# Gated spectral mix with MLP, forward and gradients: opening in blocks of four row tiles with the gate on TensorE, FFT first stage spread over the next pass, edge columns batched, loads paced

## Chip, cores, metric

The kernel runs on one core of a Trainium2 chip. The metric is the time of one execution on the device in microseconds (us).

The engines go by the names of the profile: PE multiplies and transposes matrices, DVE, ACT and POOL work on vectors, and SP issues most of the loads (SPq is its queue). PE writes its results into PSUM tiles; ACT or DVE then copies them out, which the text calls evacuation. The granted clock is the share of its full clock that PE was given.

## The reference, cut to what matters

```python
# x, grad_out: (2048, 1024) bf16;  w1: (1024, 3584);  w2: (3584, 1024)
g = sigmoid((x * gate_w).sum(-1, keepdims=True))
a = irfft2(rfft2(x) * (w_r + 1j * w_i))           # spectral branch
r = relu(x @ w1 + b1);  b = (r * r) @ w2 + b2     # MLP branch
out = g * a + (1 - g) * b                         # forward
# returned: out and the eight gradients with respect to
# x, w_r, w_i, w1, b1, w2, b2 and gate_w, for the given grad_out
```

## The kernel before

The kernel goes through five stages. In the **opening** every tile of 128 rows of `x` is turned (transposed on PE) into `xT`, its gate is computed, and `dbn = grad_out * (1 - gate)` is turned into `dbT`. The **h/dh pass** computes `ph` = w1ᵀx and `pd` = w2·db for 28 feature chunks by 4 row blocks, and turns the results for later. The **gradient GEMMs** (`pw`) have the middle of the FFT (`px`, `pv`) and its inverse stage (`pki`, `pui`) threaded between them. The **output GEMMs** (`acc`, `accg`) end the kernel. Python generators decide the interleaving: a `yield` is a place at which the builder may put another generator's instructions.

The opening took one row tile at a time, with the gate's dot product on DVE, and the FFT's first stage sat in the same generator:

```python
for i0 in range(0, NT, 4):
    ...                                           # cut: four loads xt; b1 loaded and turned
    for i in range(i0, i0 + 4):
        turned(xT, xt, i, nc.scalar.copy)         # 8 PE transposes, ACT evacuates
        nc.vector.tensor_tensor_reduce(out=junk[:], in0=xt[:], in1=gatew_bc[:], ..., accum_out=sgate[:, c_])
        nc.scalar.activation(gcol[:, c_], sgate[:, c_], ACT.Sigmoid)
        nc.vector.tensor_scalar(out=omg[:, c_], in0=gcol[:, c_], scalar1=-1.0, scalar2=1.0, ...)
        ld(out=go[:], in_=go_perm[i])
        nc.vector.tensor_scalar(out=dbn[:, i, :], in0=go[:], scalar1=omg[:, c_], ...)
        turned(dbT, dbn[:, i, :], i, nc.vector.tensor_copy)
    for i in range(i0, i0 + 4):
        one_s1(fb, cf, 0, i, xts[i - i0], kf[:])  # first FFT stage of x
    yield
for i in range(NT):                               # first FFT stage of grad_out * gate
    ...                                           # cut
    one_s1(fb, cf, 1, i, go, kg[:])
    yield
```

One unit of the first stage is a chain over three engines; the inverse stage has the same form with `pki`, `rt`, `pui`:

```python
pk = fps.tile(..., tag="ps2", bufs=2)             # PE: 8 small matmuls
nc.scalar.copy(out=ft[:], in_=pk[:])              # ACT evacuates
pu = fps.tile(..., tag="ps2", bufs=2)
column_stage(FWD, pu, ft, cf)                     # PE: 8 matmuls that read ft
nc.any.tensor_copy(out=u..., in_=pu[:])
```

All PE turns share one pair of PSUM buffers, `tag="tr", bufs=2`. The three other places that the change touches:

```python
# middle of the FFT: edge columns in matmuls of 1 or 2 columns
mm(sp[:, j, 0, :], lhsT=C, rhs=edge(0), ...)      # four such per j in spectrum, three in back
ld(out=z[:], in_=z_scr[T]...)                     # z loaded just ahead of its first use
# gradient GEMMs, at job n == 1: 16 residual loads in one burst
for t in range(NT):
    ld(out=x_[:], in_=x_perm[t])
# output GEMMs, at block k == 1: seven loads of w1T, 1 MB each, in one burst
for fc in range(0, FC, 4):
    ld(out=w1T[:, fc : fc + 4, :], in_=w1T_scr[fc : fc + 4]...)
```

Of the kernel before, what the change touches and what calls it, by code (L numbers as in the profile page):

```python
# [130 lines left out]
def kernel(  # L131
# [63 lines left out]
    ld(out=kf[:], in_=cten["kf"].ap())  # L195
    gatew_bc = pers.tile([P, D], BF16, name="gatew_bc", tag="gatew_bc")
    ld(out=gatew_bc[:], in_=gate_w.partition_broadcast(P))
    b2_bc = pers.tile([P, D], BF16, name="b2_bc", tag="b2_bc")
    cols = lambda n, w, dt=FP32: pers.tile([P] + w, dt, name=n, tag=n)
    sgate, gcol, omg, gpg, aGo, dsc = (cols(n, [NT]) for n in ("sgate", "gcol", "omg", "gpg", "aGo", "dsc"))  # L200
# [13 lines left out]
    ax_scr = [[dram.tile([P, D], FDT, name=f"ax_scr{T}_{i}") for i in range(NT)] for T in range(2)]  # L214

# [58 lines left out]
    def spectrum(fb, T, m, z, mats, sgn):  # L274
# [11 lines left out]
        sp = tps.tile([P, 2, 2, 2], FP32, name="sp", tag="tr", bufs=2)  # L286
        for j in range(2):
            re, im = main[j]
            C, Sn, N = (mats[:, j, a, :] for a in range(3))
            px = fps.tile([P, 2, H], FP32, name="px", tag="ps2", bufs=2)  # L290
            edge = lambda c_: z[:, c_, 0::H]
            mm(px[:, 0, :], lhsT=C, rhs=re, start=True, stop=False)
            mm(px[:, 1, :], lhsT=C, rhs=im, start=True, stop=False)
            kw = dict(skip_group_check=True)
            if m:

                mm(sp[:, j, 0, :], lhsT=C, rhs=edge(0), start=True, stop=False, **kw)
                mm(sp[:, j, 0, :], lhsT=(Sn if j == 0 else N), rhs=edge(1), start=False, stop=True, **kw)
                mm(sp[:, j, 1, :], lhsT=C, rhs=edge(1), start=True, stop=False, **kw)
                mm(sp[:, j, 1, :], lhsT=(N if j == 0 else Sn), rhs=edge(0), start=False, stop=True, **kw)  # L300
            else:
                mm(sp[:, j, 0, :], lhsT=C, rhs=edge(j), start=True, stop=True, **kw)
                mm(sp[:, j, 1, :], lhsT=(N if j == 0 else Sn), rhs=edge(j), start=True, stop=True, **kw)
            mm(px[:, 0, :], lhsT=Sn, rhs=im, start=False, stop=True)
            mm(px[:, 1, :], lhsT=N, rhs=re, start=False, stop=True)  # L305
            (nc.scalar.copy if j == 0 else nc.vector.tensor_copy)(out=x[:, j, :, 0:H], in_=px[:])  # L306
        V(out=x[:, :, :, 0::H], in0=sp[:], in1=sgn[:], op=ALU.mult)
        return x

    def back(fb, T, m, y, mats):  # L310

        v = fb.tile([P, 2, 2, LW], FDT, name="v", tag="v")
        sp = tps.tile([P, 2, 2], FP32, name="si", tag="tr", bufs=2)
        for j in range(2):
            C, Sn, N = (mats[:, j, a, :] for a in range(3))
            yr, yi = y[:, j, 0, :], y[:, j, 1, :]
            pv = fps.tile([P, 2, H], FP32, name="pv", tag="ps2", bufs=2)
            kw = dict(skip_group_check=True)
            mm(pv[:, 0, :], lhsT=C, rhs=yr[:, 0:H], start=True, stop=False)
            mm(pv[:, 1, :], lhsT=C, rhs=yi[:, 0:H], start=True, stop=False)  # L320
            mm(sp[:, j, :], lhsT=C, rhs=y[:, j, :, H], start=True, stop=False, **kw)
            mm(sp[:, j, 1:2], lhsT=Sn, rhs=yr[:, H : H + 1], start=False, stop=False, **kw)
            mm(sp[:, j, 0:1], lhsT=N, rhs=yi[:, H : H + 1], start=False, stop=True, **kw)
            mm(pv[:, 1, :], lhsT=Sn, rhs=yr[:, 0:H], start=False, stop=True)
            mm(pv[:, 0, :], lhsT=N, rhs=yi[:, 0:H], start=False, stop=True)
            (nc.scalar.copy if j == 0 else nc.vector.tensor_copy)(out=v[:, j, :, 0:H], in_=pv[:])
        nc.vector.tensor_copy(out=v[:, :, :, H], in_=sp[:])
        pc = fb.tile([P, 2, 2, H], FDT, name="pc", tag="pc", bufs=2)
        if m:
            V(out=pc[:, 0], in0=v[:, 0, :, 0:H], in1=v[:, 1, :, 0:H], op=ALU.add)  # L330
            vf = v[:].rearrange("p j c l -> p (j c) l")
            V(out=pc[:, 1], in0=vf[:, 3::-3, 0:H], in1=vf[:, 1:3, 0:H], op=ALU.subtract)
            V(out=pc[:, 0, 1, 0:1], in0=v[:, 0, 0, H : H + 1], in1=v[:, 1, 0, H : H + 1], op=ALU.add)
            V(out=pc[:, 1, 1, 0:1], in0=v[:, 1, 1, H : H + 1], in1=v[:, 0, 1, H : H + 1], op=ALU.subtract)
        else:
            nc.vector.tensor_copy(out=pc[:], in_=v[:, :, :, 0:H])
            nc.vector.tensor_copy(out=pc[:, :, 1, 0:1], in_=v[:, :, 0, H : H + 1])
        st(out=y_scr[T][:].rearrange("c p l -> p c l")[:, m : m + 9 : 8, :], in_=pc[:].rearrange("p j c l -> p j (c l)"))

    def fft_mid():  # L340
# [3 lines left out]
        for m in range(S2 // 2):  # L344
            am = pair_mats(fb, "amat", m)
            w = fb.tile([P, 2, 2, LW], BF16, name="w", tag="w", bufs=2)
            for c_, src_w in enumerate((A_w_r, A_w_i)):
                ld(out=w[:, :, c_, 0:W1], in_=rows2(src_w, m))
            xs = []
            for T in range(2):  # L350
                z = fb.tile([P, 2, D], FDT, name="z", tag="z", bufs=2)
                ld(out=z[:], in_=z_scr[T][:].rearrange("c p l -> p c l")[:, m : m + 9 : 8, :])
                xs.append(spectrum(fb, T, m, z, am, sgn))
                yield 8
            ap = pair_mats(fb, "apmat", m)
            wr = w[:, :, 0:1, 0:W1].to_broadcast([P, 2, 2, W1])
            wi = w[:, :, 1:2, 0:W1].to_broadcast([P, 2, 2, W1])
            for T in range(2):
# [5 lines left out]
                y = fb.tile([P, 2, 2, LW], FDT, name="y", tag="y", bufs=2)  # L364
                a_, b_ = (ALU.subtract, ALU.add) if T == 0 else (ALU.add, ALU.subtract)
                V(out=y[:, :, 0, 0:W1], in0=t1_[:, :, 0, 0:W1], in1=t2_[:, :, 1, 0:W1], op=a_)
                V(out=y[:, :, 1, 0:W1], in0=t1_[:, :, 1, 0:W1], in1=t2_[:, :, 0, 0:W1], op=b_)
                back(fb, T, m, y, ap)
                yield 8
# [13 lines left out]
            yield 4  # L383
# [48 lines left out]
    def rows_and_first_stage():  # L432

        fb, fbs = pool("f1", "right")
        cf = fb.tile(list(consts["cf"].shape), FDT, name="cf", tag="cf")
        b1row = fb.tile([FC, P], BF16, name="b1row", tag="b1row")
# [6 lines left out]

        for i0 in range(0, NT, 4):
            xts = []
            for i in range(i0, i0 + 4):
                xt = fb.tile([P, D], BF16, name="xt", tag="xt", bufs=4)
                ld(out=xt[:], in_=x_perm[i])
                xts.append(xt)
            if i0 == 0:  # L450
                ld(out=b1row[:], in_=B_b1.rearrange("(fc p) -> fc p", p=P))
                b1ps = tps.tile([P, FC], BF16, name="b1ps", tag="tr", bufs=2)
                nc.tensor.transpose(b1ps[:], b1row[:], identb[:FC, :FC])
                nc.vector.tensor_copy(out=b1col[:], in_=b1ps[:])
            for i in range(i0, i0 + 4):
                xt = xts[i - i0]
                c_ = slice(i, i + 1)
                turned(xT, xt, i, nc.scalar.copy)
                junk = fb.tile([P, D], BF16, name="junkt", tag="junkt")
                nc.vector.tensor_tensor_reduce(  # L460
                    out=junk[:], in0=xt[:], in1=gatew_bc[:], scale=1.0, scalar=0.0,
                    op0=ALU.mult, op1=ALU.add, accum_out=sgate[:, c_],
                )
                nc.scalar.activation(gcol[:, c_], sgate[:, c_], ACT.Sigmoid)
                nc.vector.tensor_scalar(out=omg[:, c_], in0=gcol[:, c_], scalar1=-1.0, scalar2=1.0, op0=ALU.mult, op1=ALU.add)
                go = fb.tile([P, D], BF16, name="go", tag="go", bufs=3)
                ld(out=go[:], in_=go_perm[i])
                nc.vector.tensor_scalar(out=dbn[:, i, :], in0=go[:], scalar1=omg[:, c_], scalar2=None, op0=ALU.mult)
                turned(dbT, dbn[:, i, :], i, nc.vector.tensor_copy)
            if i0 == 0:  # L470
                ld(out=cf[:], in_=cten["cf"].ap())
            for i in range(i0, i0 + 4):
                one_s1(fb, cf, 0, i, xts[i - i0], kf[:])
            yield
        V(out=gpg[:], in0=gcol[:], in1=omg[:], op=ALU.mult)
        for i in range(NT):
            go = fb.tile([P, D], BF16, name="go", tag="go", bufs=3)
            ld(out=go[:], in_=go_perm[i])
            kg = fb.tile([P, P], FDT, name="kg", tag="kg", bufs=2)
            nc.vector.tensor_scalar(out=kg[:], in0=kf[:], scalar1=gcol[:, i : i + 1], scalar2=None, op0=ALU.mult)  # L480
            one_s1(fb, cf, 1, i, go, kg[:])
            yield
        fbs.close()


    def mlp_in():
# [5 lines left out]
        SW = 512  # L492
        for fp in range(FC // 2):
            w1g = wb.tile([P, DC, PW], BF16, name="w1g", tag="w1g", bufs=2)
            ld(out=w1g[:], in_=w1v[:, :, fp * PW : (fp + 1) * PW])
            h2S = wb.tile([P, NT, PW], BF16, name="h2S", tag="stg", bufs=3)
            dhS = wb.tile([P, NT, PW], BF16, name="dhS", tag="stg", bufs=3)
            for f2 in range(2):
# [288 lines left out]
```

## Time and profile before

| | before |
|---|---|
| time, median of 4 runs | 1483.88 us (1483.01 to 1484.96) |
| span of the profiled execution | 1482.7 us |
| PE work (weight loads times pace) | 1405.9 us |
| lost by PE | 77 us |

"PE work" is the number of PE weight loads in a stretch times the pace at which that kind of matmul follows the last one; the prediction derives the paces. "Lost" is the length of a stretch less its PE work. The page's row of busy times, shares and instruction counts says this of before:

```profile
PE 1426.7 (96%) x8333; PEld 723.4 (49%) x8482; DVE 669.2 (45%) x1319; ACT 438.2 (30%) x564; POOL 219.9 (15%) x395
```

There are 8482 weight loads (PEld) but only 8333 recorded matmuls, which is why the loads are counted.

### The profile page before, as it was taken

How to read it: one execution, taken by the hardware profiler on the slowest of the kernel's cores; microseconds unless marked ns; L12 is line 12 of the kernel's file. 1: busy time of each engine (PE TensorE's matmuls, PEld its weight loads, DVE VectorE, ACT ScalarE, POOL GpSimd, SP SyncE). 2: the span in 40 equal slices, each digit the busy share in tenths (PEclk: the TensorE clock that was granted, in tenths of full speed). 3: DMA queues.
4: the chain of work that ended last, by engine and by line, in shares of the span. 5: the costliest groups of instructions: out<-in, count | busy, mean ns of one | idle time of the engine just before them, and what ended most of it. 6: DMA issues, size and time to landing. Idle time of an engine off the chain costs nothing. (4 is left out here: it accounts for less than half of the span.)

```text
span 1482.7 us, 20756 instructions
## 1 busy us (share of the span) xinstructions
PE 1426.7 (96%) x8333; PEld 723.4 (49%) x8482; DVE 669.2 (45%) x1319; ACT 438.2 (30%) x564; POOL 219.9 (15%) x395
## 2 busy tenths in 40 slices
PE   6899999999999997999999999999989999999998
PEld 4655555555555553444444444444445544444443
DVE  7953343343433335555554443211455655562222
ACT  5854444444444331322322222333222200000000
POOL 1321111111111111111101122111101100000000
PEclk9999999999999999999999999999999999999999
DMA  7565555555555747555546544944785554664430
GB/s 258 165 210 185 184 181 179 171 178 166 180 171 177 280 135 282 185 187 181 167 155 187 186 181 164 336 153 146 240 285 164 161 155 128 182 185 126 122 112 22
DMA packets 157194, 267.45 MB, mean 180 GB/s; under 512 B 10652, under 2 KB 90538, under 8 KB 155306
## 3 DMA queue, kind: packets, MB, share of 16 engines
q1 hardware_dynamic: 122890, 147.59, 31.5%
q0 software_dynamic: 34208, 118.53, 23.8%
q8 instruction: 66, 1.08, 0.3%
q14 instruction: 30, 0.25, 0.1%
HBM read 147.57 MB, written 118.51 MB: 179 GB/s over the span
## 5 line engine op out<-in xcount | busy, mean ns | idle before, releaser
L520 PE MATMUL pd<-dbT,w2T 128*128 128x512 bf16 x883 | 211.5, 379 | 1.7 <-DVE dhT L521 1.0
L514 PE MATMUL ph<-xT,w1g 128*128 128x512 bf16 x850 | 211.6, 379 | 1.4
L521 DVE SCALAR_TENSOR_TENSOR dhT<-pd,rT 128x512 bf16<-128x512 f32 x112 | 77.5, 692 | 275.9 <-PE pd L520 257.8
L677 PE MATMUL acc<-w,hblk 128*128 128x512 bf16 x874 | 198.4, 381 | 1.2
L616 PE MATMUL pw<-grp,res 128*128 128x512 bf16 x870 | 198.2, 379 | 1.3
L604 PE MATMUL pw<-dbn,grp 128*128 128x512 bf16 x872 | 195.5, 379 | 1.2
L715 PE MATMUL accg<-w1Tr,hblk 128*128 128x512 bf16 x878 | 192.6, 379 | 0.9
L516 ACT ACTIVATE rT<-ph,b1col 128x512 bf16<-128x512 f32 x112 | 77.0, 688 | 215.0 <-PE ph L514 215.0
L715 PEld LDWEIGHTS <-hblk 128*128 128x128 bf16 x896 | 87.7, 98 | 105.7
L520 PEld LDWEIGHTS <-w2T 128*128 128x128 bf16 x896 | 87.4, 98 | 105.6 <-DVE w2T L507 3.8
L604 PEld LDWEIGHTS <-grp 128*128 128x128 bf16 x896 | 87.5, 98 | 105.3 <-issue 0.2
L677 PEld LDWEIGHTS <-hblk 128*128 128x128 bf16 x896 | 87.3, 98 | 98.9 <-issue 1.1
L616 PEld LDWEIGHTS <-res 128*128 128x128 bf16 x896 | 87.0, 98 | 99.1
L514 PEld LDWEIGHTS <-w1g 128*128 128x128 bf16 x896 | 83.2, 98 | 72.9
L608 ACT CAST wo<-pw 128x512 bf16<-128x512 f32 x56 | 32.7, 584 | 154.4 <-PE pw L604 141.3
L410 DVE TENSOR_TENSOR tt<-e 128x512 f16<-128x512 f16 x32 | 13.6, 425 | 139.8 <-ACT e L408 139.3
L306 DVE CAST x<-px 128x1024 f16<-128x1024 f32 x16 | 19.6, 1225 | 120.7 <-PE px L305 120.6
L621 ACT CAST wo<-pw 128x512 bf16<-128x512 f32 x56 | 32.8, 585 | 132.2 <-PE pw L616 125.1
L517 ACT ACTIVATE h2T<-rT 128x512 bf16<-128x512 bf16 x112 | 70.5, 630 | 3.5
L716 DVE TENSOR_TENSOR gxo<-accg,g 128x512 bf16<-128x512 f32 x32 | 22.1, 691 | 107.4 <-PE accg L715 103.9
L404 ACT CAST rt<-pki 128x1024 f16<-128x1024 f32 x32 | 32.5, 1015 | 78.0 <-PE pki L402 78.0
L678 DVE SCALAR_TENSOR_TENSOR ot<-acc,omg,af 128x512 bf16<-128x512 f32 x32 | 24.0, 750 | 58.7 <-PE acc L677 54.0
(177 smaller groups left out, 1636.0 us busy)
## 6 DMA issues: line engine op xcount, KB each, us to landing
h2T_scr<-h2T POOLq DMA_DIRECT2D x28, 512.0 KB, 3.4
dhT_scr<-dhT POOLq DMA_DIRECT2D x28, 512.0 KB, 4.4
h_scr<-h2S POOLq DMA_DIRECT2D x14, 1024.0 KB, 8.1
dh_scr<-dhS POOLq DMA_DIRECT2D x14, 1024.0 KB, 10.5
grp<-h_scr SPq DMA_DIRECT2D x7, 2048.0 KB, 9.4
grp<-dh_scr SPq DMA_DIRECT2D x7, 2048.0 KB, 8.6
hblk<-h2T_scr SPq DMA_DIRECT2D x8, 1792.0 KB, 9.0
hblk<-dhT_scr SPq DMA_DIRECT2D x8, 1792.0 KB, 9.1
```

What stands on the lines that cost most here:

```text
L404: nc.scalar.copy(out=rt[:], in_=pk[:])
L514: mm(ph[:], lhsT=w1g[:, dc, fs], rhs=xT[:, dc, ss], start=(dc == 0), stop=(dc == DC - 1))
L516: nc.scalar.activation(rT[:], ph[:], ACT.Relu, bias=b1col[:, fc : fc + 1])
L517: nc.scalar.activation(h2T[:, ss], rT[:], ACT.Square)
L520: mm(pd[:], lhsT=w2T[:, ec, :], rhs=dbT[:, ec, ss], start=(ec == 0), stop=(ec == DC - 1))
L521: STT(out=dhT[:, ss], in0=pd[:], scalar=2.0, in1=rT[:], op0=ALU.mult, op1=ALU.mult, accum_out=gb1part[:, fc, sb : sb + 1],)
L604: mm(pw[:], lhsT=cur[:, t, fb_ * P : (fb_ + 1) * P], rhs=dbn[:, t, hf * H : (hf + 1) * H], start=(t == 0), stop=(t == NT - 1),)
L608: nc.scalar.copy(out=wo[:, hf * H : (hf + 1) * H], in_=pw[:])
L616: mm(pw[:], lhsT=xr[t][:, d_ * P : (d_ + 1) * P], rhs=cur[:, t, :], start=(t == 0), stop=(t == NT - 1),)
L621: nc.scalar.copy(out=wo[:], in_=pw[:])
L677: mm(acc[:], lhsT=cur[:, fc, t2 * P : (t2 + 1) * P], rhs=w2[:, fc, cs], start=(fc == 0), stop=(fc == FC - 1))
L715: mm(acc[:], lhsT=cur[:, fc, t2 * P : (t2 + 1) * P], rhs=w1T[:, fc, cs], start=(fc == 0), stop=(fc == FC - 1))
```

## The change

Its intent is to fill the places in which PE waits: start on `x` at once, give the opening of each block the matmuls of the MLP as neighbours, move the FFT's first stage to where the GEMMs are dense, spend fewer instructions on edge columns, and keep bulk loads from blocking urgent ones. The core of the diff, with cuts marked:

```diff
# opening: a block of four tiles, the gate dot as 1-column matmuls into PSUM
+            for i in range(i0, i0 + 4):
+                ld(out=xt[:], in_=x_perm[i])
+                turned(xT, xt, i, nc.scalar.copy)
+            ...                                   # cut: b1 and gate_w turned together
+            yield
+            pg = tps.tile([P, 4], FP32, name="pg", tag="tr", bufs=2)
+            for i in range(i0, i0 + 4):
+                for dc in range(DC):
+                    mm(pg[:, i - i0 : i - i0 + 1], lhsT=xT[:, dc, ...], rhs=gwcol[:, dc : dc + 1], ...)
+            nc.scalar.activation(gcol[:, c_], pg[:], ACT.Sigmoid)
+            nc.vector.tensor_scalar(out=omg[:, c_], ...)
+            for i in range(i0, i0 + 4):
+                ld(out=go[:], in_=go_perm[i])
+                nc.vector.tensor_scalar(out=dbn[:, i, :], in0=go[:], scalar1=omg[:, i : i + 1], ...)
+                turned(dbT, dbn[:, i, :], i, nc.vector.tensor_copy)
+            yield
# h/dh pass: first chunk pair ordered by row block, yields before ph and before pd; dhT/h2T 3 buffers (cut)
# driver: two steps of the pass after each half block, then the first stage at 0.4 units a step
+    for i0 in range(0, NT, 4):
+        next(units), next(units)
+        next(row_gen)
+        next(units), next(units)
+        next(row_gen, None)
+    mixed = spread(units, first, 0.4)
# FFT middle: z, matrices and weights of pair m+1 loaded while pair m runs; edges of both spectra
# gathered by POOL and done in 4 + 4 matmuls a pair; back once a pair (cut)
+            if m + 1 < S2 // 2:
+                nxt = inputs(m + 1)
# paced loads: each one waits for an instruction of the GEMM
+                        if n in (2, 3):
+                            after(ld(out=x_[:], in_=x_perm[len(xr)]), last)
-            if k == 1:
-                for fc in range(0, FC, 4):
-                    ld(out=w1T[:, fc : fc + 4, :], ...)
+                if t % 2 == 1 and t // 2 < FC // 4:
+                    after(ld(out=w1T[:, fc : fc + 4, :], ...), last)
```

## The prediction

> **What bounds the kernel now.** I read the table by stretches first. Its columns: stretch and its length, then busy time (and instructions) of PE, PE weight loads, DVE, ACT and POOL, then granted clock, DMA share, GB/s.
>
> ```profile
> 9.25:100.00 90.75, 78.87 (x732) 54.72 (x740) 73.14 (x185) 65.03 (x82) 26.45 (x59) 1.00 0.62 199
> 100.00:560.00 460.00, 452.26 (x3083) 246.47 (x3134) 173.59 (x397) 194.23 (x262) 84.21 (x145) 1.00 0.57 184
> 560.00:600.00 40.00, 30.86 (x151) 14.07 (x153) 26.18 (x31) 6.58 (x10) 4.98 (x7) 0.91 0.85 291
> 600.00:920.00 320.00, 318.31 (x1629) 146.87 (x1660) 165.51 (x253) 89.54 (x114) 50.99 (x83) 1.00 0.53 173
> 1080.00:1120.00 40.00, 35.79 (x187) 17.93 (x189) 20.81 (x51) 8.10 (x8) 3.78 (x7) 0.91 0.70 230
> 1200.00:1475.00 275.00, 273.68 (x1249) 124.38 (x1273) 116.14 (x172) 0.00 (x0) 12.76 (x22) 1.00 0.44 129
> ```
>
> PE bounds nearly everything; the clock dips in two stretches only. Busy time still flatters PE: a 512-column matmul is shown as 379 ns long, but they start closer together, as two rows of PE's timeline show (start, length, operation):
>
> ```profile
> 88.50 1.89 PE L514 MATMUL ph<-xT,w1g 128*128 128x512 bf16 x8
> 590.67 0.59 PE L292 MATMUL px<-z,amat 128*128 128x512 f16 x1 [8.38 <-DMA z<-z_scr]
> 591.05 0.63 PE L293 MATMUL px<-z,amat 128*128 128x512 f16 x1
> 602.53 0.17 PE L321 MATMUL si<-y,apmat 128*128 128x2 f16 x1
> 602.55 0.16 PE L322 MATMUL si<-y,apmat 128*128 128x1 f16 x1
> 602.58 0.16 PE L323 MATMUL si<-y,apmat 128*128 128x1 f16 x1
> 1097.57 1.04 PE L402 MATMUL pki<-ki,r 128*128 128x128 f16 x8 [3.81 <-DMA r<-y_scr]
> ```
>
> Eight in 1.89 us: (1.89-0.38)/7 = 0.216 us each. A 128-column matmul or transpose goes at 0.056 us (eight in 0.61, one 0.22), a one- or two-column edge matmul at about 0.027 us (starts 602.53, .55, .58). So I count work with these paces and the number of weight loads, which the trace records completely (it misses about 150 matmuls). Total: 6 x 896 + 256 of 512 columns = 5632 x 0.2158 = 1215; 64 column stages of 8 matmuls, 0.98 each = 63; 512 + 1600 small ones x 0.0558 = 118; 216 edge ones x 0.027 = 6; column sums 4. Sum **1406 us of PE work**, so the span of 1482.7 loses 77 us. By stretches, length minus work counted the same way: start 9.3; 9.25-100 loses 19.9 (128 x 0.2158 + 17 x 0.98 + 475 x 0.0558 = 70.8 of 90.75); 100-560 loses 13.6 (work 446.4); 560-600 loses 11.2; 600-920 only 0.2; 920-1080 6.0; 1080-1200 9.7; then nothing until the tail, 7.1. The change can win only from these 77.
>
> The waits of PE (who waits, for whom, us in total, times, longest) name the large ones:
>
> ```profile
> PE b1ps L453 <- DMA b1row<-in_B_b_dram: 9.2, 1, 9.2
> PE px L292 <- DMA z<-z_scr: 8.4, 1, 8.4
> PE pu L255 <- ACT ft L235: 5.8, 12, 1.4
> PE pki L402 <- DMA r<-y_scr: 3.8, 1, 3.8
> PE ptr L537 <- DVE dhT L521: 3.7, 19, 0.2
> ```
>
> and the DMA-issuing queue's timeline shows why z was late: fifteen residual loads stood ahead of it.
>
> ```profile
> 562.40 14.11 SPq L596 DMA_DIRECT2D res<-in_A_x_dram  x15
> 583.49 0.98 SPq L352 DMA_DIRECT2D z<-z_scr  x2
> ```
>
> **What the Trainium skill says.** "TensorE: Matmul & The Clock Gate", Back-to-back issue gap: a matmul starts N/2.4 + 2.5 ns after the last, and Wait — 56ns, not 53.3ns? puts the floor for tiny ones near 25 ns. The trace agrees (216 and 27 ns). The same page, under HAM oscillation: a PE idle for over about 3.4 us drops to half clock. The trace agrees: after the 8.38 us wait the first two matmuls start 0.38-0.43 us apart instead of 0.216. So a long DMA wait costs more than its length: some 1.8 us here (3.6 us at half rate), and some 2.6 after the wait at 1097. "DMA: Bandwidth & Descriptors", Issuing engines are not separate DMA queues: all transfers share 16 engines and interleave. The trace agrees: the seven w1T loads of 1 MB issued together took a median of 14.7 us to land, and the r loads issued among and after them came late. "Perfetto Trace Analysis", Identifying the Most-Contended Engine: PE busy share is no measure of the distance to the roof. Agreed: 96% busy, 1406/1482.7 = 95% by work, and in the opening 87% busy against 78% by work.
>
> **The change, part by part.**
>
> *Edges.* Before, a row pair needs 16 edge matmuls in spectrum (8 for m = 0) and 12 in back: 7 x 16 + 8 + 8 x 12 = 216. After: 4 + 4 per pair, 64. 152 x 0.027 = **-4.1 us**, in a saturated stretch, so all of it on the path. The small copies go to POOL, 16% busy there.
>
> *Gate dot on PE.* 16 tiles x 8 one-column matmuls = 128 x 0.027 = **+3.5 us** of PE; it frees DVE of 16 x (1.22 + 0.08) = 21 us in the opening, where DVE is 73 of 91 us busy.
>
> *Start.* PE stood behind the b1 transpose; b1 was issued at 4.00, eighth in line, after kf and the 256 KB broadcast of gate_w. Afterwards the x tiles come almost first: the four x tiles landed 0.67 us apart, the first at 7.04; without the broadcast I put it at about 5.2. **-4.0 us.**
>
> *Opening.* PE work there: 32 turned tiles x 0.446 = 14.3, gate 3.5, eight ph+pd pairs x 3.45 = 27.6, w2/w1 turns 1.8, transposes of h and dh 3.6: 51 us. ACT needs 16 x 1.01 + 8 x 1.34 + 2 = 29, DVE 16 x (0.48 + 0.69) + 8 x 0.77 + 11 x 0.69 = 33; neither binds, only the chains do. First block: x turned and copied by ACT at 1.01 each until about 10.3; ph 1.7; gate, sigmoid, omg about 1.2; then DVE 4 x 1.17 until about 19-20, with only one ph to fill it: loses about 5 after the start. The other three have the neighbour block's matmuls to fill, about 2.5 each, 7.5. Sum about 13-14 against 19.9: **-6 us**. This is the softest number.
>
> *First stage spread.* 32 units instead of 16 fall into the h/dh pass. A trace breakdown of 100-560 by pair of neighbours gives 4.7 us lost around 15 units there (pu behind ft, ph behind pk), 0.31 each, the rest 8.9 over 460 us. After: 8.3 + 32 x 0.31 = 18.2 against 13.6: **+4.6 us**. The units' own PE work only moves.
>
> *Residual loads paced, z prefetched.* z leaves the queue without 4 MB ahead of it, and its first reader comes after four blocks of the gradient GEMM (14 us) instead of two. Of the 11.2 about 2 stay: **-9.2 us**.
>
> *w1T paced.* The 3.8 us wait for r and its 2.6 us of cold clock go: **-6.4 us**. But in the new order y is stored one step later before the inverse stage reads it, and paced loads block the queue behind a wait: **+2.5 us** allowed for.
>
> Sum: -4.1 + 3.5 - 4.0 - 6 + 4.6 - 9.2 - 6.4 + 2.5 = -19.1; I allow 2-3 us more for h2T/dhT buffers (two to three) and smaller staging stores, which shorten waits in the pass. 1483.9 - 22 = **1462 us**, 1.5% faster.
>
> **Rivals.** (1) *A new wait takes the old one's place.* z is now 16 KB per partition per buffer pair and may lie where the pass's staging tiles lie; then it loads only once those are stored, as the residuals did (that queue waited 46 us on ph). For: the buffers do overlap in time. Against: 14 us of GEMM cover. It would give back 5-10: about 1470. (2) *The opening stays chained*: sigmoid, omg, scale, transpose, copy in series for four tiles, and the pair of PSUM buffers is shared by x, dbn, the gate and the w turns. For: PE waits of 0.3-1.6 us on dbn and xT in the old opening. Against: DVE now has slack. It gives 1468-1472. (3) *The scheduler fills better than I think*: opening loses 7, the pass no more than now: about 1450. (4) *Batched back* (four 2-bank results in a row over two buffers, evacuated in 1.0 on ACT and 1.2 on DVE): could stall 0.5 us x 8 = 4; against: 600-920 lost 0.2 us with the same buffers. POOL is not a rival: 15% busy.
>
> **Range and chances.** Worst plausible sum, rivals 1 and 2 together, is about 1473; the best, rival 3 with all waits gone, 1448. Over 2% means under 1454.2, which needs the opening and the pass both to go well: 0.2. Slower by 2% has nothing in the profile to speak for it.
>
> **What would show it.** Right: PE's first matmul near 5 us; no wait of PE on z or r over 2 us, and clock 1.00 in both transitions; edge matmuls 64; PE work 1405; loss in the h/dh pass up to about 18; first 60 us losing about 14 after the start. Wrong: any new DMA wait of over 3.4 us with a clock dip, idle PE at gate or dbn in each opening block, or PE waits in the spectrum stretch. The prediction is wrong as a whole if the opening loses as much as before, or if the scheduler orders first-stage units so that they stall the pass by over 0.6 us each.

## The result, and the profile after

| | before | after |
|---|---|---|
| time, median of 4 runs | 1483.88 us | 1471.10 us (1470.82 to 1471.35) |
| span of the profiled execution | 1482.7 us | 1469.2 us |
| PE work | 1405.9 us | 1405.3 us |
| lost by PE | 77 us | 64 us |

The ratio is 0.9913, with a 95% interval of 0.9896 to 0.9931: 0.9% faster. A ratio here is the mean time of one kernel's runs over that of the other's of the same rounds, so it is not quite the ratio of the medians quoted. The time is inside the predicted range, but the gain is 12.8 us where 22 had been predicted.

The same row of the page after the change:

```profile
PE 1437.6 (98%) x8458; PEld 722.2 (49%) x8458; DVE 650.0 (44%) x1275; ACT 438.2 (30%) x554; POOL 259.1 (18%) x463
```

There are 24 weight loads fewer: 152 edge matmuls went and 128 of the gate came. PE's busy time went up by 11 us although its work fell by 0.6. Here no matmul record is missing, and before about 150 were: busy time is no measure of this change.

The table by stretches of the changed kernel (columns as in the prediction: stretch and length, then PE, PE weight loads, DVE, ACT, POOL, granted clock, DMA share, GB/s). The opening now ends near 73 us, because the first stage has left it:

```profile
4.66:73.40 68.74, 57.81 (x595) 38.51 (x596) 32.08 (x77) 30.43 (x40) 6.53 (x14) 0.98 0.73 233
73.40:567.50 494.10, 491.98 (x3441) 269.43 (x3439) 199.28 (x471) 231.01 (x297) 116.76 (x220) 1.00 0.57 189
567.50:600.00 32.50, 32.08 (x155) 14.39 (x152) 24.08 (x28) 6.56 (x10) 10.86 (x16) 1.00 0.73 244
600.00:920.00 320.00, 317.68 (x1517) 143.64 (x1516) 166.17 (x252) 88.87 (x114) 73.17 (x116) 1.00 0.55 184
1080.00:1200.00 120.00, 119.12 (x647) 58.52 (x646) 72.41 (x170) 22.66 (x23) 10.81 (x20) 1.00 0.63 203
```

Both transitions now have the full clock (0.91 before) and a busy PE. The loss, stretch by stretch, in us (the first three rows compare stages, whose times have shifted):

| stage | lost before | lost after | difference | predicted |
|---|---|---|---|---|
| start, until PE's first matmul | 9.3 | 4.7 | -4.6 | -4.0 |
| opening (9.25-100; 4.66-73.4) | 19.9 | 20.8 | **+0.9** | **-6** |
| h/dh pass (100-560; 73.4-567.5) | 13.6 | 16.6 | +3.0 | +4.6, less 2 to 3 for buffers |
| transition (560-600; 567.5-600) | 11.2 | 0.5 | -10.7 | -9.2 |
| 600-920, FFT middle | 0.2 | 3.6 | +3.4 | 0 |
| 920-1080, inverse stage | 6.0 | 6.6 | +0.6 | - |
| 1080-1200 | 9.7 | 2.9 | -6.8 | -6.4 and +2.5 |
| tail after the last `accg` | 7.1 | 8.5 | +1.4 | - |

With the 0.6 us of work saved (-4.1 + 3.5, as predicted) the differences sum to -13.4; the spans differ by 13.5.

The waits of PE after (who waits, for whom, us in total, times, longest):

```profile
PE pt L485 <- DVE dbn L514: 5.6, 6, 2.2
PE pt L485 <- DMA xt<-in_A_x_dram: 5.3, 2, 4.7
PE pw L666 <- DVE row L633: 1.5, 1, 1.5
```

The long waits for `b1row`, `z` and `r` are gone; the 4.7 is the start itself. What has come to the top are transposes of the opening that wait for `dbn` (1.6 us, once, before). PE's timeline of the opening (start, length, operation, idle time before it and what ended it) shows the first two blocks:

```profile
11.08 3.55 PE L576 MATMUL ph<-xT,w1g 128*128 128x512 bf16 x8
14.47 0.94 PE L505 MATMUL pg<-gwcol,xT 128*128 128x1 bf16 x32
17.62 2.67 PE L485 MATMUL pt<-identb,dbn 128*128 128x128 bf16 x24 [2.21 <-DVE dbn L514]
...
34.27 1.07 PE L485 MATMUL pt<-identb,dbn 128*128 128x128 bf16 x16 [1.39 <-DVE dbn L514]
```

`ph` runs first, at half clock (3.55 us for what takes 1.89 later), and only behind it comes the gate dot `pg`. Nothing then stands between `pg` and the transposes that need its result. The timeline of all engines shows what lies in that gap on ACT:

```profile
15.38 1.28 ACT L509 ACT_TABLE_LOAD   x1
16.67 0.17 ACT L509 ACTIVATE gcol<-pg 128x4 f32<-128x4 f32 x1
```

And the wait costs again, by the clock. It is only 2.2 us long, but between 14.4 and 17.8 PE is busy for 1.19 us in all, the tiny gate matmuls included. The prediction's rule, a PE idle for over 3.4 us, does not cover this case. The stretch just after it (same columns as the table above) is at half clock:

```profile
17.80:21.20 3.40, 3.16 (x31) 2.81 (x29) 2.93 (x6) 0.00 (x0) 0.00 (x0) 0.51 0.68 212
```

At the transition, where before the queue held 15 residual loads ahead of `z`, the issuing queue and PE after the change read:

```profile
566.84 0.98 SPq L380 DMA_DIRECT2D z<-z_scr  x2
```

```profile
582.10 0.38 PE L295 MATMUL px<-z,amat 128*128 128x512 f16 x1
```

`z` is asked for at 566.8 instead of 583.5, its first reader starts without any wait, and at full clock.

### The profile page after: what moved, and what is told of

Its sections match the earlier page's. It is cut to its first block, busy times and chain, and to the rows that moved or that the text cites. A ratio compares the mean times of both kernels' runs of the same rounds, so it can differ in the third digit from the quotient of the medians.

```text
span 1469.2 us, 20972 instructions
## 1 busy us (share of the span) xinstructions
PE 1437.6 (98%) x8458; PEld 722.2 (49%) x8458; DVE 650.0 (44%) x1275; ACT 438.2 (30%) x554; POOL 259.1 (18%) x463
## 3 DMA queue, kind: packets, MB, share of 16 engines
q8 instruction: 66, 1.08, 0.3%
## 4 chain that ended last, share of the span: by engine, by line
PE 54%; issue 35%; POOL 4%; DVE 2%; DMA 1%; ACT 0%; POOLq 0%; DVEq 0%; ACTq 0%
PE pd L584 12%; PE ph L576 12%; PE pw L666 11%; PE pw L682 6%; PE ptr L599 3%; PE pu L260 3%; PE ptw L549 2%; POOL ax_scr L461 1%; POOL out_dram L688 1%; DMA out_dram<-wo 1%; PE pk L238 1%; POOL out_dram L784 1%; POOL out_dram L747 1%; DVE dhT L585 1%; PE px L295 0%
## 5 line engine op out<-in xcount | busy, mean ns | idle before, releaser
L576 PE MATMUL ph<-xT,w1g 128*128 128x512 bf16 x896 | 227.3, 381 | 0.2 <-ACT xT L486 0.2
L454 DVE TENSOR_TENSOR tt<-e 128x512 f16<-128x512 f16 x32 | 13.6, 425 | 122.6 <-ACT e L452 122.0
L601 DVE COPY stg<-ptr 128x1024 bf16<-128x1024 bf16 x84 | 55.4, 687 | 14.3 <-PE ptr L599 14.3
L244 ACT CAST u<-pu 128x1024 f16<-128x1024 f32 x32 | 41.7, 1303 | 41.4 <-PE pu L260 41.4
```

The source lines that it names most:

```text
L576: mm(ph[:], lhsT=w1g[:, dc, fs], rhs=xT[:, dc, ss], start=(dc == 0), stop=(dc == DC - 1))
L601: eng(out=stg[k_, sb][:, :, fs], in_=ptr[:])
```

## The experiments

The theory after the comparison: the transition, the w1T loads, the edges and the first stage behave as predicted, and the opening failed because the gate dot stands **behind** `ph` on PE, so that `ph` can't cover the chain gate, sigmoid, scaling. The rivals: the gate on PE is itself the cost; the chain through `dbn` is unavoidable and bounds the gain; the repairs at the transitions come from something other than the pacing.

Every edit is to the changed kernel (1471.10 us, ratio 0.9913). All had three rounds against the kernel before, whose medians in the three calls were 1484.27, 1485.3 and 1484.45. The calls ran on different chips, so I give two comparisons with the changed kernel: the difference of medians, and the difference of the two ratios times 1484. They differ by up to 1.4 us, so I read nothing into a difference smaller than that.

| run | median us | ratio to before, 95% | against changed: medians, ratios |
|---|---|---|---|
| e1_w1t_burst | 1477.32 | 0.9949 (0.9932-0.9966) | +6.2, +5.3 |
| e2_res_burst | 1477.03 | 0.9945 (0.9930-0.9960) | +5.9, +4.7 |
| e3_gate_dve | 1470.36 | 0.9906 (0.9891-0.9920) | -0.7, -1.0 |
| e4_dbt_unscaled | 1468.01 | 0.9889 (0.9874-0.9904) | -3.1, -3.6 |
| e5_gate_first | 1461.56 | 0.9842 (0.9823-0.9862) | -9.5, -10.5 |
| e6_split_first | 1463.42 | 0.9859 (0.9840-0.9877) | -7.7, -8.0 |
| e7_split_inverse | 1462.66 | 0.9847 (0.9825-0.9870) | -8.4, -9.8 |
| e8_late_turn | 1463.71 | 0.9855 (0.9835-0.9875) | -7.4, -8.6 |
| e9_edges_added | 1474.42 | 0.9932 (0.9917-0.9947) | +3.3, +2.8 |
| c1_all_four | 1437.53 | 0.9684 (0.9670-0.9699) | -33.6, -34.0 |
| c2_more | 1440.25 | 0.9698 (0.9682-0.9714) | -30.9, -31.9 |
| c3_warm | 1435.97 | 0.9674 (0.9659-0.9688) | -35.1, -35.5 |

### e1: w1T in one burst again

```diff
+            if k == 1:
+                for fc in range(0, FC, 4):
+                    ld(out=w1T[:, fc : fc + 4, :], ...)
-                if t % 2 == 1 and t // 2 < FC // 4:
-                    fc = 4 * (t // 2)
-                    after(ld(out=w1T[:, fc : fc + 4, :], ...), last)
```

> The changed kernel with the seven w1T loads issued together again. Theory of the prediction (pacing them is what removed the wait for r): PE waits 3 to 5 us on r near 1080 again, a clock dip follows, about 6 us slower than the changed kernel, near 1477. Rival (the later order of the inverse stage moved r away from them anyway): within 1 us of 1471, no PE wait on r over 1 us.

It came out 6.2 us slower, and the wait that had gone is back in the view of PE's waits:

```profile
PE pki L446 <- DMA r<-y_scr: 4.0, 1, 4.0
```

The clock is at half for 3.4 us after it, and 1080-1200 loses 8.3 us instead of 2.9. The prediction's -6.4 for this part stands. The opening, which the edit does not touch, lost 1.3 us more in this profile, because its clock came later (see "Left open").

### e2: residual loads in one burst again

```diff
                 column_sums(wb, mps, "pw", acc, out_7)
+                for t in range(NT):
+                    ...
+                    ld(out=x_[:], in_=x_perm[t])
-                        if n in (2, 3):
-                            after(ld(out=x_[:], in_=x_perm[len(xr)]), last)
```

> The changed kernel with the 16 residual loads in one go again, z still prefetched and still first read after four blocks of the gradient product. Theory A (pacing the residuals is what let z in): z queues behind them again, PE waits 6 to 9 us on z at about 582 and the clock dips, 8 to 11 us slower, 1479 to 1482. Theory B (the prefetch and the later first use suffice): PE wait on z under 2 us, 1471 to 1473.

It is 5.9 us slower, in between the two theories. Queue and PE of this run:

```profile
565.26 8.74 SPq L662 DMA_DIRECT2D res<-in_A_x_dram  x11
```

```profile
586.71 0.61 PE L295 MATMUL px<-z,amat 128*128 128x512 f16 x1 [3.93 <-DMA amat<-c_amat]
```

Eleven loads stand ahead of `z` and the matrices, PE waits 3.93 us, and the clock is at half for 6.8 us from 585.1 on, so that PE runs at half clock from 586.7 to 591.9; the transition loses 7.4 us instead of 0.5. With the burst, then, the loss is 7.4; before the change it was 11.2. By this stretch pacing is worth 6.9 of the 10.7 us gained there (5.9 by the medians). The other 3.8 belong to the parts of the change that are still in this kernel; prefetching `z` and its later first use are the likely ones, not separated.

### e3: gate dot on DVE again

```diff
+                if i == 0:
+                    ld(out=gatew_bc[:], in_=gate_w.partition_broadcast(P))
+                nc.vector.tensor_tensor_reduce(
+                    out=dbn[:, i, :], in0=xt[:], in1=gatew_bc[:], ..., accum_out=sgate[:, i : i + 1])
-            pg = tps.tile(...);  32 matmuls into pg
-            nc.scalar.activation(gcol[:, c_], pg[:], ACT.Sigmoid)
+            nc.scalar.activation(gcol[:, c_], sgate[:, c_], ACT.Sigmoid)
```

> The changed kernel with the gate dot back on the Vector engine, 16 reductions of 1.3 us, everything else as changed. Intent of the change (the dot on PE frees the opening): 3 to 8 us slower, 1474 to 1479. Rival, which I now hold (in the new opening DVE is busy 32 of 69 us, the x tiles are there a block early, and the dot on PE stands in the chain behind ph): the sigmoid no longer waits for ph, 128 matmuls of 0.027 us go, 2 to 6 us faster, 1465 to 1469.

No difference (-0.7 us), so neither forecast came true. PE has 3.5 us less work, and loses 3.5 us more by 73.4 us. The waits of PE show that effects of both kinds are in this run. Those on `dbn` fell from 5.6 to 1.1 us. But the load of `gate_w` for DVE now stands among the first `x` tiles, and the second wait for `x` grew from 0.6 to 2.0 us; and work that stands behind the reductions on DVE is waited for anew (1.7 us on `dhT`, 1.1 on `gwcol`, 3.2 instead of 0.7 on `dbT` by transposes). In sum, with the load that it needs, the gate dot on DVE is neither better nor worse in this order of instructions; the run does not isolate the place of the dot.

### e4: dbT turned from grad_out unscaled (wrong results on purpose)

```diff
-                turned(dbT, dbn[:, i, :], i, nc.vector.tensor_copy)
+                turned(dbT, go, i, nc.vector.tensor_copy)
```

> Wrong results on purpose: dbT is turned from grad_out itself, not from the scaled dbn, so the turning no longer waits for gate, sigmoid, omg and scale; amount of work unchanged. If that chain is what the opening loses (waits of 1.0 to 2.2 us of PE on dbn in each block), 6 to 10 us faster, 1461 to 1465, opening loss from 20.8 down to 11 to 14. If the two transposition buffers and the evacuation of x and dbT are what it loses, 0 to 3 us faster.

The gradients of x, w1 and b1 are wrong by design. With PE's transposes freed from the data of the gate chain, only 3.1 us are gained, about what the rival said at most. I had taken this as the bound on what any repair of the gate could give. That was a mistake, which the waits of PE show:

```profile
PE pt L485 <- ACT gcol L509: 1.2, 2, 1.0
```

The transposes of `go` do not read the gate, yet they wait for the sigmoid: `pg` sits in one of the two "tr" buffers until the sigmoid has read it, and `pg` itself still stands behind `ph`. That is the smaller part. The larger is that the transposes also wait for DVE to copy them out: the waits of PE on `dbT` sum to 5.6 us in the opening, against 1.4 in the changed kernel, while those on `dbn` (5.6) are gone. The largest group, and DVE's timeline, which shows why:

```profile
PE pt L485 <- DVE dbT L486: 2.4, 5, 0.7
```

```profile
17.24 0.17 DVE L510 TENSOR_SCALAR omg<-gcol 128x4 f32<-128x4 f32 x1 [4.12 <-ACT gcol L509]
17.44 0.49 DVE L514 TENSOR_SCALAR dbn<-go,omg 128x1024 bf16<-128x1024 bf16 x1
17.85 0.68 DVE L486 COPY dbT<-pt 128x1024 bf16<-128x1024 bf16 x1
```

DVE runs its instructions in the order shown, and each copy stands behind a scaling that still waits for the gate. The run took the gate out of PE's data and left it in the buffer and in DVE's order.

### e5: gate before the block's ph

```diff
-            yield
             pg = tps.tile(...);  32 matmuls;  sigmoid;  omg
+            yield
             for i in range(i0, i0 + 4):               # dbn and dbT
```

> The changed kernel with gate dot, sigmoid and omg placed ahead of the block's first ph instead of behind it, so that ph covers the chain up to the scaled dbn. Since the run with the unscaled dbT bounds that chain at 3 us: 2 to 3 us faster than the changed kernel, 1468 to 1469, PE's waits on dbn under 2 us in total instead of 5.6. Rival (the x tiles' copies on ACT delay the dot as much): within 1 us of 1471.

One `yield` moved, 9.5 us gained where 2 to 3 had been expected. PE's timeline of the second block:

```profile
26.70 0.35 PE L504 MATMUL pg<-gwcol,xT 128*128 128x1 bf16 x8 [0.18 <-ACT xT L486]
26.91 1.89 PE L576 MATMUL ph<-xT,w1g 128*128 128x512 bf16 x8
28.64 1.06 PE L485 MATMUL pt<-identb,dbn 128*128 128x128 bf16 x16
```

`ph` now runs while sigmoid and scaling are under way, and the transposes of `dbn` start without a wait. No wait on `dbn` is left, and the clock does not drop at 17.8. The loss by block, from PE's first matmul on: 10.4, 3.8, 4.1, 2.4 us in the changed kernel; 6.4, 2.2, 1.8, 1.7 here. The opening up to 73.4 loses 12.0 instead of 20.8. That is 8.8 of the 9.5; the other stretches change by -2.8 and +2.0.

### e6: first FFT stage in two steps

```diff
         nc.scalar.copy(out=ft[:], in_=pk[:])
+        yield
         pu = fps.tile(...)
-    mixed = spread(units, first, 0.4)
+    mixed = spread(units, first, 0.8)
```

> The changed kernel with each first-stage unit cut in two, pk with its evacuation in one step, the column stage pu in the next, a step later. The trace of the changed kernel loses 5.3 us in 30 places where pu follows ph before ACT has finished ft (0.18 us each). If that latency is the cost of spreading the stage over the pass: these 5 us go, 1466 to 1468, pass loss from 16.6 to 11 to 13. Rival (the cost lies in the shared PSUM buffers and the turns of dhT): no gain, 1470 to 1473.

7.7 us gained. With other matmuls between `pk` and `pu` while ACT copies `ft`, the pass loses 12.0 instead of 16.6. The largest single group in the changed kernel's pass had been the gap between a `ph` matmul and the `pu` after it, 5.3 us in 30 places. The rest lies where the edit changes nothing: 1.2 us in the tail, and in 600-920, for which see "Left open".

### e7: inverse stage in two steps

```diff
                 nc.scalar.copy(out=rt[:], in_=pk[:])
+                yield 1
                 pu = fps.tile(...)
-    todo = 1 + 6 * (S2 // 2) + NT
+    todo = 1 + 6 * (S2 // 2) + 2 * NT
```

> The changed kernel with each unit of the inverse stage cut in two in the same way (pki in one step, pui in the next). 920 to 1200 loses 9.4 us now, as it did before without the wait for r, about 0.29 us in each of 32 places where pui follows a dense matmul. If it is again the ACT latency: 6 to 9 us faster, 1462 to 1465. Rival (DMA or DVE bound there): within 2 us of 1471.

8.4 us gained; 920-1200 loses 0.4 instead of 9.4. PE's timeline of one row tile in the changed kernel, and in this one:

```profile
1000.16 0.61 PE L446 MATMUL pki<-ki,r 128*128 128x128 f16 x8
1000.61 1.24 PE L682 MATMUL pw<-grp,res 128*128 128x512 bf16 x5
1001.96 1.17 PE L260 MATMUL pui<-ci,rt 128*128 128x512 f16 x8
```

```profile
1001.45 0.61 PE L446 MATMUL pki<-ki,r 128*128 128x128 f16 x8
1001.89 3.62 PE L683 MATMUL pw<-grp,res 128*128 128x512 bf16 x15
1005.35 1.16 PE L260 MATMUL pui<-ci,rt 128*128 128x512 f16 x8
```

In the changed kernel five `pw` matmuls (5 x 0.216 = 1.08 us) are too few for ACT's copy: from the start of `pw` to that of `pui` 1.35 us pass, 0.27 too many. In e7 there are 16 (one record is missing; the weight loads show 16), which take 3.46 us, and `pui` starts 3.46 us after `pw`: nothing is lost. Adding up such excess gaps between starts in 920-1200 of the changed kernel gives 32, one for each of the 32 row tiles, 8.5 us in all, and only one is over 0.3 us. The view of waits lists one of them. The change did not touch this loss.

### e8: turn of dhT held back behind the next unit's ph

```diff
+        held = []                      # turn_out() holds the body of the old loop
-                    for k_, src in enumerate((h2T, dhT)):  ... turn, evacuate, store
+                    turn_out(0, h2T, ...)
+                    held.append((1, dhT, ...))             # for fp > 0
                 nc.scalar.activation(h2T[:, ss], rT[:], ACT.Square)
+                let_go()
```

> The changed kernel with the turn of dhT put off until behind the next unit's ph, so that it does not follow its own scaling on DVE at once. The pass loses about 10 us around the 52 turns of dhT (0.2 us each). If DVE's latency is the cause: 6 to 9 us faster, 1462 to 1465. Rival (the transposition buffers are held up by their copies): 0 to 2 us.

7.4 us gained; the pass loses 10.4 instead of 16.6. In the changed kernel the changeovers from `ph` or `pk` to the turn of `dhT`, which needs DVE's evacuation of `pd`, had cost 7.2 us in 39 places (with the 14 turns of `h2T`, 9.5 us in 53). In the profiled run, the fastest of the four, the opening too lost 2.3 us less and 600-920 2.2 us less, neither of which the edit was meant to touch (see "Left open").

### e9: edge matmuls added

```diff
+            for _ in range(10 if j else 9):
+                mm(o, lhsT=C, rhs=src[j][0], start=True, stop=True, skip_group_check=True)
```

> The changed kernel with 19 more eight-column edge matmuls per row pair, 152 in all, as many as the change took out (their results are overwritten, the outputs stay right). At 0.027 us each in a saturated stretch: 4.1 us slower, 1475. If the weight loads cost 0.05 or more each: 8 us. If they hide in gaps: under 2 us.

152 extra edge matmuls, as many as the change took away, cost 3.3 us (2.8 by ratios) where 152 x 0.027 = 4.1 were counted. The size is right to within 1.3 us.

### c1: e5, e6, e7 and e8 together

> The changed kernel with the four edits of the last runs together: gate first, both stages cut in two, dhT turned late. Their gains over the changed kernel were 9.5, 7.7, 8.4 and 7.4 us, 33 together. If they stand in different places of the chain they add: about 1438 to 1442, over 2% below the kernel before. If they share causes (the pass holds the first stage and the turns): 1444 to 1450.

The edit is the four diffs above. The gains add: 9.5 + 7.7 + 8.4 + 7.4 = 33.0, measured 33.6. The fit is partly chance. Cut at instructions (from the last turn of `dbn` to the last turn or `pd`), the pass loses 17.2 us in the changed kernel, 11.9 in e6, 10.2 in e8 and 1.4 here: 15.8 gained where the two gave 12.3. Against that, what e6 gained in the tail (1.2) and e8 in the opening (about 2) is not repeated here. It is 3.2% faster than the kernel before, with correct results. The pass loses 1.6 us instead of 16.6, 920-1200 loses 0.4 instead of 9.4, the opening 12.8 instead of 20.8.

### c2 and c3: two more attempts at the opening

```diff
# c2 = c1 and:
+    nc.scalar.activation(gcol[:, 0:1], ones_f[:], ACT.Sigmoid)     # load the table at the start
-            pt = tps.tile([P, DC, P], ..., tag="tr", bufs=2)       # for dbT
+            pt = fps.tile([P, DC, P], ..., tag="ps2", bufs=2)
# c3 = c2 and:
+        heat(9)                # 512-column matmuls on zeros while PE waits for x
                 turned(xT, xt, i, nc.scalar.copy)
+                if i0 == 0:
+                    heat(2)
```

> The four edits, and besides: a sigmoid issued at the start so that its table (1.28 us of ACT between the first gate dot and its sigmoid) is loaded early, and the turns of dbn through the PSUM buffers of the FFT, which stand empty in the opening. In the run with the gate first PE still waits 0.3 to 0.35 us on dbT in each block and about 0.5 us for clearing: 2 to 3 us below the four edits. Rival (those waits are hidden by ph now): 0 to 1 us.

> The same, and idle PE is kept busy with 17 dummy matmuls of 512 columns from 1 us on, until the x tiles are turned. In the changed kernel the clock is granted fully only from 14.4 us, and PE runs its first 7 us of work at half rate. If the cold clock is what the start costs: full clock from about 5 to 8 us, ph 0.216 us apart, 2 to 4 us below the run without. Rival (ACT's copies and the landing of x, w1g and w2r set the pace until 11 us): within 1 us.

c2 missed: it is 2.7 us slower than c1, not 2 to 3 faster. The opening loses 16.4 instead of 12.8, with a new wait of PE on `dbn` of 2.3 us and half clock from 61.2 to 64.6. The order of instructions changed with the buffers. The trace shows where it hurt in the last block: the sigmoid starts at 56.6, but DVE computes `omg` only at 59.5, behind pieces of the first FFT stage (`uv`) that waited for their load until 58.5; in c1 `omg` comes at 57.4. The early table was not tried alone. c3 against c2, whose only difference is the 17 dummy matmuls, gains 4.3 us. Its first turn of `dbn` starts at 13.1 us where c2's starts at 15.9, 2.8 us earlier; it also lacks c2's half clock at 61.2, so the 4.3 are not the warm start alone. PE's timeline of c3:

```profile
1.21 4.02 PE L497 MATMUL heat<-dbn 128*128 128x512 bf16 x9 [1.21 <-DVE dbn L492]
...
11.39 1.89 PE L610 MATMUL ph<-xT,w1g 128*128 128x512 bf16 x8
```

The clock is full from 6.7 us instead of 16.9, and the first `ph` takes 1.89 us where it took 3.55 in the changed kernel. c3 is the fastest kernel, 1435.97 us, but by only 1.6 us over c1, which is simpler.

## Why the prediction was right or wrong

**Right in direction and in most terms.** The edges (-4.1 and +3.5) left the work as counted, and e9 gave 3.3 for the 4.1. The start was -4.6 for -4.0. The transition was -10.7 for -9.2, and e2 shows pacing as its larger part. The w1T loads were -6.8 for -6.4, confirmed by e1. Spreading the first stage cost +3.0 net for a term of +4.6, and e6 shows that the mechanism named, `pu` behind `ft`, was the one. Rival 1, a new wait on `z`, did not come. The +2.5 set aside for `y` and for the queue behind the paced loads was hardly needed.

**Wrong: the step "Opening", -6 us; measured +0.9.** Two of its terms failed. "First block: ... with only one ph to fill it: loses about 5 after the start" lost 10.4. "The other three have the neighbour block's matmuls to fill, about 2.5 each, 7.5" lost 3.8 + 4.1 + 2.4 = 10.3. My series for the first block itself put `ph` ahead of the gate and then counted it as the filling of the chain behind the gate (and its "13-14" is 12.5 when added up). In the changed kernel `ph` precedes the gate dot, so the filling was spent before the chain began. e5 shows this as the cause: moving one `yield` brings the opening to 12.0, near the predicted 12.5 (5 + 7.5). The first block also ran at half clock until 14.4 and again from 17.8 to 21.2, while my sum used full pace; c3 against c2 shows what warming PE early is worth in its own surroundings, 2.8 us by the first turn of `dbn`. The prediction had named its own sign of being wrong as a whole, "if the opening loses as much as before", and that sign came. Rival 2, "the opening stays chained", which put the time at 1468 to 1472, is what came: 1471.1. That the time lies in the range is owed to this rival having been allowed for and to terms that went better than forecast (5.0 us, below); the sum itself missed by 9 us.

**Smaller misses.** The term for the first stage rests on a misreading: the eight gaps of "ph behind pk" before the change, 0.22 us each, are each one missing matmul record, as the weight loads at 218.04 and 218.09 show. A unit lost 0.17 us before (2.5 us in 15 places, `pu` behind `ft`) and not 0.31, and 0.18 after (5.3 us in 30); also, the rest of the pass is 8.9 us in one line of the prediction and 8.3 in the next. The allowance of "2-3 us more for h2T/dhT buffers" did not show as a separate gain; at most it is the difference between +4.6 and +3.0. 600-920 lost 3.4 more, of which 1.5 is one wait for `row` of the column sums, and rival 4 (batched back) explains part at most. The tail lost 1.4 more until the last small store landed. As a balance against the predicted terms: worse are the opening (6.9), 600-920 (3.4), the tail (1.4), the pass with its buffer allowance of 2.5 (0.9) and 920-1080 (0.6), together 13.2; better are the start (0.6), the transition (1.5) and 1080-1200 with its allowance (2.9), together 5.0. The difference, 8.2 us, is that between the predicted 21.6 (19.1 + 2.5) and the 13.4 found.

**Where the larger gain was.** Most of it was in no long wait. What e6, e7 and e8 work on is, in the changed kernel, 84 gaps in the pass (15.2 us) and 32 in 920-1200 (8.5 us), all but two of 0.3 us or less, where PE stands behind an evacuation on ACT or DVE; c1 leaves three of the 84. The view of waits ranks them low or leaves them out, but the loss per stretch has them, before the change too (13.6, 6.0 and part of 9.7 us), and the prediction only carried them over.

**Left open.** The clock of the opening is not the same from profile to profile. Seven profiles have the same opening code (the changed kernel, e1, e2, e6, e7, e8, e9): full clock first comes at 9.1 us in e8, at 14.4 in the changed kernel and at 23.4 in e7, and the opening to 73.4 loses 18.5 to 22.4 us. e5's 12.0 lies well outside, but about 2 us of the gain of any one profile can come from this. In all seven the clock is at half, still or again, just after PE's first wait on `dbn` (2.2 us); e4, e5 and c1, which lack this wait, keep the full clock once they have it (from 14.0 to 16.5 us on).

What 600-920 loses seemed to depend on the schedule elsewhere: 3.6 us in the changed kernel, 1.2 to 1.5 in e5, e6 and e8, whose code there is the same. Most of that comes from cutting at fixed times while the kernel gets faster. Cut at the first `px` and the last `pv` or edge matmul, it is 3.4 in the changed kernel and 2.4 to 2.8 in e5, e6 and e8, so at most 1 us of their gains lies there. The share of prefetch and of later use in the transition was not separated, nor that of the early table load in c2 and c3.

## What to carry to other kernels

Put the start of a latency chain (here gate, sigmoid, scaling) ahead of the dense work that is to cover it: the same instructions in the other order cost 9.5 us. Where work is threaded into a GEMM, make producer, evacuation and consumer separate steps, so that something lies between them; e6, e7 and e8 gained 23.5 us, some 20 of them (4.6, 9.0 and 6.2 in their stretches) in stalls too short to stand out as waits. Bulk loads that nobody needs yet should be tied to the progress of the GEMM, since a burst delays the urgent load behind it and a wait of some 4 us then costs again through the clock.

## What the Trainium skill lacked or had wrong

- "TensorE: Matmul & The Clock Gate", Back-to-back issue gap, gives a sustained pace of about 131 ns a matmul at 512 columns and about 81 ns at 128 for streams of weight load and matmul, and calls its formula (216 and 56 ns) the isolated gap only, a limit that the prediction left out. Here the formula is what streams of weight load and matmul show: eight 512-column ones in 1.89 us are 216 ns each, and eight transposes or 128-column matmuls in 0.61 us are 56 ns each.
- "ScalarE: Activation LUTs", What ACT_TABLE_LOAD costs, adds a drain of about 1380 ns to a load of about 1283 ns. The load agrees (1.28 us at 15.38), but it starts 0.02 us after the end of ACT's previous instruction, and the sigmoid starts 1.29 us after the load began, so no such drain shows here.
- No page that I found says that a tiny PSUM result placed in a ring shared with large ones blocks the ring until it is read. Here the four columns of `pg` held one of two buffers, and transposes that do not depend on them waited 1.0 us for the sigmoid (e4).
- No page that I found has the time of one kernel with and without dummy matmuls that warm PE at its start. Here 17 dummy matmuls from 1.21 us on gave full clock at 6.7 instead of 16.9 us, and the first turn of `dbn` started 2.8 us earlier (c3 against c2); c3 is 1.6 us faster than c1, which has neither them nor c2's edits.
